# Attention with rotary embedding and a mixture of experts: the token lists' matrices are spread over four head pairs, built on ScalarE alone, with chunk counts summed by TensorE and token numbers taken from a constant table

## The chip, the cores and the metric

The kernel runs on one core of a Trainium2 chip. The metric is the device time of one execution in microseconds (us). A core has TensorE (PE; its weight loads are listed apart as PEld), VectorE (DVE), ScalarE (ACT), GpSimd (POOL) and SyncE (SP, which here only issues DMAs). Each engine works through its own instructions in the order in which the program gives them, and waits on semaphores for the other engines.

## The reference

Eight batches of 576 tokens go through attention with 8 heads of 64 columns; the result, 4608 tokens of 512 columns, goes through a mixture of experts in which each token visits one of 8 experts.

```python
q_rot, k_rot = rotate(q), rotate(k)                 # rotary embedding
scores = q_rot @ k_rot.T / sqrt(64)
attn = softmax(scores); x = attn @ v                # (8, 8, 576, 64) -> (4608, 512)
logits = x @ w_gate; e_idx = argmax(logits, axis=1)
gate_w = softmax(logits)[e_idx]; eom = sigmoid(x @ w_output_gate)
for e in range(8):
    mask = e_idx == e
    h = relu(x[mask] @ w1[e])
    out[mask] = gate_w[mask] * eom[mask, e] * (h @ w2[e])
```

## The kernel before, in words

**Attention.** Two heads form a pair; a batch has 4 pairs, the program 32. A pair is worked through in nine steps, one for each block of score rows (`STEPS`): steps 0 and 1, 2 and 3, 5 and 6, 7 and 8 are issued together, step 4 alone. A step multiplies the scores on TensorE (`score`, L509), takes the row peak and copies them out of PSUM on VectorE (`peak`, L518, tile `pm`), takes the exponential with its sum on ScalarE (`exp`, L525, tile `pm`) and turns them on VectorE (`turn`, L531 and L533, tile `pt`). One pair later the values are multiplied (L555, tile `acc`, one buffer for the whole kernel), ScalarE copies them out (`evict`, L562 to L564, tile `ac`), TensorE turns them back (`back`, L570, again into `acc`), and VectorE divides them into the rows of tokens (`divide`, L582, tile `xb`). GpSimd prepares the queries and keys of coming pairs: a multiplication by the rotary table (L460, two a pair), an addition (L464) and the low halves (L473).

**What sets the order.** A table of events gives each side task an offset in steps from the start of its pair, and a number that orders the tasks of one step; `step` issues a step's scores, peaks and exponentials, the turns of earlier steps, and then the tasks due. Nothing is reordered later: a task stands in its engine's queue between the exponentials, peaks or score products of the steps around it.

**The place of a token.** When a batch's four pairs are done, `place` finds for its tokens (5 chunks of 128, the last half full) the expert, the gate value, and the token's place in the expert's list. It runs 20 steps and more after the start of the batch's last pair, beside the attention of later pairs. `s0` to `s8` find the expert as a one-hot row per token (tile `oh`, a bf16 copy `ohb`). `add0` and `add` make sums of `ohb` over the chunks before (tile `ohs`). `s14` multiplies both by constant matrices on TensorE, which gives the rank of each token within its expert. `s15` to `s17` split the place into a row number `hr` and a column number `lo`. `ones(c)` and `places(c)` build for each chunk two matrices, `ro` (128x288, one where the row number agrees) and `pl` (128x128, the token's number where the column number agrees); on ScalarE each takes two activations, a square and a clipped difference (L736 and L737, L747 and L748). `s20` multiplies the five pairs of matrices into one bank of `acc` (L758), `s21` copies that out (L764, tile `lc`), and `s22` adds it to the lists on GpSimd. For the last batch all of this runs on VectorE, with pieces issued between the products of the experts.

Before the change, batches 0 to 5 have their ten matrices within offsets 25 to 40 (`ROWS`, `PLACES`), which is within a pair and a half; `pl` of chunks 0 to 2 is built on ScalarE (`TURNED` is 3), of chunks 3 and 4 on GpSimd (L750). Batch 6 (`ahead`) is placed while the attention ends.

**Experts.** Tokens are gathered by list in slots of 256 or 128, multiplied by both weight matrices of their expert (L1133, L1125, L1175) and scattered. This starts when attention ends and keeps TensorE busy to the end.

Of the kernel before, what the change touches and what calls it, by code (L numbers as in the profile page):

```python
# [22 lines left out]
E, FF = 8, 1024  # L23
# [49 lines left out]
C_E8, C_MASK, C_TOK, C_EB, C_SL, C_TRI, C_ONE, C_ROW = range(8)  # L73


def list_rows(nb):
# [13 lines left out]
    return n0, n2, max(min(E, most - 2 * p) + 2 * max(0, p - n2) for p in range(most // 2 + 1))  # L90


def const_table(nb):
# [11 lines left out]
    parts = [e8, mask, tok, eb, sl, tri, one, row]  # L105
# [160 lines left out]
class Attention:  # L266


    def __init__(self, tc, nb, pools, cc, ident, ii, first, trib, oneb, cnt, zero, qk, v, xd, row, lists):
# [32 lines left out]
        for i, pr in enumerate(self.pairs):  # L302
            g, b = 9 * i, i // NP
            fs = {"lasts": pr.lasts, "den0": pr.den0, "den1": pr.den1, "den2": pr.den2, "evict": pr.evict, "back": pr.back,
                  "newxb": lambda pr=pr, b=b: newxb(b) if pr.hp == 0 else None}
            fs["divide"] = lambda pr=pr, b=b: pr.divide(xbs[b])
            for t, n in ((slice(0, 1), "0"), (slice(1, 2), "1"), (slice(0, 2), "")):
                fs[f"mult{n}"] = lambda pr=pr, t=t: pr.mult("P", t)
                fs[f"add{n}"] = lambda pr=pr, t=t: pr.add("P", t)
                fs[f"hi{n}"] = lambda pr=pr, t=t: pr.high(t)  # L310
                fs[f"lo{n}"] = lambda pr=pr, t=t: pr.low("P", t)
            for t in range(2):
                fs[f"load{t}"] = lambda pr=pr, t=t: pr.load(t)
                fs[f"loadv{t}"] = lambda pr=pr, t=t: pr.loadv(t)
            for k, (b0, b1) in enumerate(PIECES):
                fs[f"av{k}"] = lambda pr=pr, b0=b0, b1=b1: [pr.values(j) for j in range(b0, b1)]
            for name, o, k in [*PREP.get(i, PREPARED), *EVENTS]:
                at(g + o, k, fs[name])
            if i % NP == NP - 1:
                fs = place(tc, (px, px2, small), self.pairs, b, NT, cc, trib, oneb, cnt, xbs, xd, row, lists, self.later)  # L320
# [70 lines left out]
class Pair:  # L391
# [194 lines left out]
def number(NT, b):

    m = NT // S // 2 * S
    return float(b * S - m + (b * S >= m))


def place(tc, pools, pairs, b, NT, cc, trib, oneb, cnt, xbs, xd, row, lists, later):
# [8 lines left out]
    T = {}  # L601

    def new(n, sh, dt=F32, **k):
        T[n] = p2.tile(sh, dt, tag=n, name=f"{n}{b}", **k)
        return T[n]

    sign = -1.0 if number(NT, b) < 0 else 1.0
    CE = [P, NCH, E]
    LO, LG = slice(0, E), slice(E, 2 * E)

# [30 lines left out]
    def s6():  # L641
# [18 lines left out]
    def add(c):  # L660
# [57 lines left out]
    def s17():  # L718
# [23 lines left out]
    def places(c):  # L742

        if c == 0:
            new("pl", [P, NCH, P], F32R, bufs=1)
        if not last and c < TURNED:
            nc.scalar.activation(T["pl"][:, c, :], row[:, 0:P], AF.Square, bias=T["lo"][:, c:c + 1], scale=-1.0)  # L747
            nc.scalar.activation(T["pl"][:, c, :], T["pl"].bitcast(F32)[:, c, :], AF.Relu, bias=T["tok"][:, c:c + 1], scale=T["tik"][:, c:c + 1])  # L748
            return
        V.tensor_scalar(T["pl"][:, c, :], row[:, 0:P], T["lo"][:, c:c + 1], T["tok"][:, c:c + 1], op0=ALU.is_equal,  # L750
                                op1=ALU.mult)

    def s20():

        T["ls"] = psum(4 if ahead else 5, 128, lists.shape[1])
        for c in range(NCH):
            m = QR if c == 4 else P
            nc.tensor.matmul(T["ls"], T["pl"][0:m, c, :], T["ro"][0:m, c, :], start=(c == 0), stop=(c == 4), skip_group_check=True)  # L758

    def s21():  # L760
        if last:
            nc.vector.tensor_tensor(out=lists, in0=lists, in1=T["ls"], op=ALU.subtract if sign < 0 else ALU.add)
            return
        nc.scalar.copy(new("lc", [P, lists.shape[1]], bufs=1), T["ls"])  # L764

    def s22():
        nc.gpsimd.tensor_tensor(out=lists, in0=lists, in1=T["lc"], op=ALU.subtract if sign < 0 else ALU.add)

    def both(f, c):
        return lambda: (f(), add(c))  # L770

    no = lambda: None
    if last:
        later += [lambda i=i: store(i) for i in range(3)]
        run = lambda *fs: lambda: [f() for f in fs]
        return [s0, run(s1, s2), s3, run(s4, s5), run(s6, s7), run(s8, add0), both(s9, 1), lambda: [add(c) for c in (2, 3, 4)],
                run(s10, s11, s12), run(s13, base), no, no, no, no, s14, no, s14b, run(s15, s16, s17)] + [
                lambda c=c: (ones(c), places(c)) for c in range(NCH)] + [no, no, s20, no, s21, no]

    def adds(*cs):  # L780
        return lambda: [add(c) for c in cs]
# [541 lines left out]
```

## Time and profile before

| | us |
|---|---|
| median of 3 runs (lowest, highest) | 974.33 (972.52, 975.57) |
| the profiled execution | 973.69 |
| its span, first to last instruction | 971.9 |

| engine | busy us | share of the span | instructions |
|---|---|---|---|
| PE | 910.4 | 94% | 14413 |
| DVE | 759.1 | 78% | 1353 |
| ACT | 650.2 | 67% | 1353 |
| POOL | 542.2 | 56% | 519 |

The shares are means over two stages with different limits. Attention lasts from the start to about 490 us, the experts from there to the end. [...] The number of tokens in a list depends on the data, which is the same in all runs.

### The profile page before, as it was taken

To read this page: it belongs to the slowest core of one execution; us is meant where nothing else is said; L and a number is where in the kernel's file an instruction comes from. 1 tells how busy PE (TensorE), PEld (TensorE's weight loads), DVE (VectorE), ACT (ScalarE), POOL (GpSimd) and SP (SyncE) were. 2 spreads that over 40 slices of the span, in tenths; PEclk is the share of its full clock that TensorE was granted. 3 is DMA by queue.
4 is the path that set the end of the run, shared out by engine and by line. 5 is a ranking of instruction groups with operands and counts; after the bars stand their busy time and mean duration, and the time that the engine had idled before them with its cause. 6 is when DMAs were issued, how large, how long until landed. Compare 5 with 4: busy or idle time off the path is not lost.

```text
span 971.9 us, 34146 instructions
## 1 busy us (share of the span) xinstructions
PE 910.4 (94%) x14413; PEld 787.9 (81%) x14413; DVE 759.1 (78%) x1353; ACT 650.2 (67%) x1353; POOL 542.2 (56%) x519
## 2 busy tenths in 40 slices
PE   4989989989899899889899999999999999999997
PEld 3768778767777777777788998999889998999986
DVE  6889989999899998999779767657665767658562
ACT  4767787897978878798765454446654756457561
POOL 5897889898898988898411222142514215142140
PEclk9999999999999999999999999999999999999999
DMA  6543563573564555562578877668786868868650
GB/s 234 198 168 132 195 223 138 196 253 114 217 209 177 204 195 180 182 225 91 209 297 281 305 238 236 210 201 303 258 288 223 301 201 279 283 225 286 197 202 23
DMA packets 57821, 208.38 MB, mean 214 GB/s; under 512 B 7946, under 2 KB 8252, under 8 KB 57664
## 3 DMA queue, kind: packets, MB, share of 16 engines
q1 hardware_dynamic: 49920, 183.78, 54.7%
q0 software_dynamic: 6464, 21.26, 5.9%
q8 instruction: 115, 1.88, 0.8%
q10 hardware_dynamic: 1280, 1.11, 0.3%
q14 instruction: 42, 0.34, 0.1%
HBM read 186.06 MB, written 22.43 MB: 215 GB/s over the span
## 4 chain that ended last, share of the span: by engine, by line
PE 43%; issue 4%; DVE 3%; ACT 2%; POOL 1%; DMA 1%; POOLq 0%; ACTq 0%; DVEq 0%
PE py L1175 19%; PE ph L1133 18%; PE ph L1125 3%; PE mtp L1098 1%; DVE wl L1092 1%; DMA out<-y,2idx 1%; ACT wh L1090 1%; PE acc L555 1%; PE htp L1160 0%; PE sc L509 0%; POOL kq L473 0%; POOL wl L1092 0%; POOLq L1254 0%; DVE ht L1150 0%; POOL out L1180 0%
## 5 line engine op out<-in xcount | busy, mean ns | idle before, releaser
L525 ACT ACTIVATE pm<-pm,m 128x576 f32<-128x576 f32 x288 | 221.7, 771 | 89.5 <-DVE pm L518 86.9
L1092 DVE TENSOR_TENSOR wl<-wr,wh 128x1024 fp32r<-128x1024 f32 x172 | 216.0, 1270 | 37.1 <-ACT wh L1090 34.2
L518 DVE TENSOR_SCALAR_CACHE_REDUCE pm<-sc 128x576 f32<-128x576 f32 x288 | 206.9, 750 | 26.3 <-PE sc L509 21.3
L555 PE MATMUL acc<-pt,v 32*64 32x160 f32 (+1 forms) x9216 | 197.2, 295 | 18.7 <-DVE xb L582 5.8
L1175 PE MATMUL py<-wh,ht 128*128 128x512 f32 x640 | 213.7, 399 | 0.0
L1133 PE MATMUL ph<-xt,wh 128*128 128x256 f32 x1088 | 197.3, 282 | 0.8 <-issue 0.4
L555 PEld LDWEIGHTS acc<-pt,v 32*64 32x64 f32 x9216 | 157.2, 131 | 44.1 <-issue 21.6
L1090 ACT CAST wh<-wr 128x1024 fp32r<-128x1024 f32 x184 | 187.8, 1049 | 0.0
L509 PE MATMUL sc<-kq 64*128 64x288 f32 x1536 | 156.6, 319 | 18.1 <-ACT kq L470 9.5
L1133 PEld LDWEIGHTS ph<-xt,wh 128*128 128x128 f32 x1088 | 168.6, 188 | 3.2 <-DVE xt L1114 1.8
L460 POOL TENSOR_TENSOR raw<-raw,rt 128x1152 f32<-128x1152 f32 x62 | 164.6, 2655 | 0.0
L509 PEld LDWEIGHTS sc<-kq 64*128 64x128 f32 x1536 | 118.7, 191 | 51.5 <-DVE pm L518 19.8
L1133 PE MATMUL ph<-xt,wl 128*128 128x256 f32 x544 | 153.5, 282 | 0.1
L1175 PEld LDWEIGHTS py<-wh,ht 128*128 128x128 f32 x640 | 120.4, 188 | 25.0
L533 DVE STREAM_TRANSPOSE pt<-pm 128x1152 f32<-128x1152 f32 x96 | 131.8, 1373 | 0.1
L1175 PE MATMUL py<-wl,ht 128*128 128x512 f32 x320 | 125.7, 393 | 0.0
L1180 POOL DMA_INDIRECT out<-y,2idx x24 | 28.1, 1169 | 163.8 <-ACT y L1189 103.5
L1149 ACT ACTIVATE ht<-ph 128x512 fp32r<-128x512 f32 x68 | 40.6, 597 | 109.0 <-PE ph L1133 106.6
L1133 PEld LDWEIGHTS ph<-xt,wl 128*128 128x128 f32 x544 | 102.2, 188 | 1.0 <-issue 0.5
L1150 DVE SCALAR_TENSOR_TENSOR ht<-ph,ht 128x512 fp32r<-128x512 f32 x68 | 46.9, 690 | 69.4 <-ACT ht L1149 65.3
L473 POOL TENSOR_TENSOR kq<-raw,kq 128x1152 fp32r<-128x1152 f32 (+1 forms) x33 | 82.5, 2500 | 10.9 <-ACT kq L470 10.7
L464 POOL TENSOR_TENSOR raw<-raw 128x1152 f32<-128x1152 f32 (+1 forms) x33 | 82.4, 2496 | 1.6
(251 smaller groups left out, 1112.0 us busy)
## 6 DMA issues: line engine op xcount, KB each, us to landing
wr<-in_w SPq DMA_DIRECT2D x184, 512.0 KB
raw<-in_qk SPq DMA_DIRECT2D x64, 576.0 KB
v<-in_v SPq DMA_DIRECT2D x64, 576.0 KB
xd<-xb SPq DMA_DIRECT2D x16, 640.0 KB
xd<-xb SPq DMA_DIRECT2D x8, 160.0 KB
rt<-in_rope ACTq DMA_DIRECT2D x1, 576.0 KB
xg<-xd,2idx POOLq DMA_INDIRECT x24, 6.5
out<-y,2idx POOLq DMA_INDIRECT x24, 3.9
```

Source lines behind the costliest of these rows:

```text
L460: self.eng(eng).tensor_tensor(out=rv, in0=rv, in1=rt, op=ALU.mult)
L464: self.eng(eng).tensor_tensor(out=r, in0=r, in1=self.sides(self.raw, t, 1, x), op=ALU.add)
L473: self.eng(eng).tensor_tensor(out=self.sides(self.kq, t, 0, x), in0=self.sides(self.raw, t, 0, x), in1=self.sides(self.kq.bitcast(F32), t, ...
L509: self.nc.tensor.matmul(self.ps[i][:, a, :HS], st, self.kq[r, mov, x], start=(n == 0), stop=(n == 2))
L518: self.nc.vector.tensor_scalar(self.halves(i), self.ps[i][:, :, :HS], 1.0, FAR, op0=ALU.mult, op1=ALU.min, accum_out=self.m[i])
L525: self.nc.scalar.activation(self.pc[i], self.pc[i], AF.Exp, bias=self.m[i], scale=-1.0, accum_out=self.z[:, zi:zi + 1])
L533: self.nc.vector.transpose(out=self.pt[:, c:c + 6:5, :], in_=self.pc[units])
L555: nc.tensor.matmul(self.acc[h * D:h * D + D, a, o:o + 32 * n], self.v[r, h, j, :], self.pt[r, u:u + n, 32 * j:32 * j + 32], start=(j == 0) ...
L1090: self.nc.scalar.copy(wh, r)
L1092: eng.tensor_tensor(out=wl, in0=r, in1=wh.bitcast(F32), op=ALU.subtract)
L1133: nc.tensor.matmul(ph[:, f, :], st[:, dc, fs], mv[:, dc, :], start=(n == 0), stop=(n == 11))
L1175: self.nc.tensor.matmul(py[h], st[:, f, hs], mv, start=(f == 0 and n == 0), stop=(f == 7 and n == 2))
```

## The change

Six edits, all in `place`, its tables of offsets and the constant table. First, a batch has a kind: `free` (batches 0 to 3), `late` (4), `early` (5), `ahead` (6), or it is the last (7). For the kinds free and late the matrices are spread: offsets 29 to 58 for free batches, 28 to 51 for the late one; the lists are multiplied two pairs later (free) or one pair later (late). Kinds early and ahead keep their offsets. Second, for free and late batches `pl` of all five chunks is built on ScalarE. Third, TensorE sums the chunk counts: five products of one chunk each with the matrix of ones, with the chunk's one-hot row broadcast over all later chunks, take the place of `add0`, `add` and one product. Fourth, token numbers `tok` and their negatives `tik` come from the constant table. Fifth, the one-hot rows are written as bf16 at once, into one tile `hot` shared by all batches (tile `score` likewise), and rows without a token are masked by the table `e8` and a ninth column of 0.5 in `score`. Sixth, `s3` to `s7` and `base` stand one to three steps later.

```diff
-LISTED = 44
-TURNED = 3
-ROWS, AHEAD, PLACES = (26, 29, 31, 35, 40), (26, 29, 29, 31, 31), (25, 29, 31, 34, 38)
+LISTED, LATE = 44, 9
+ROWS = {"ahead": (26, 29, 29, 31, 31), "early": (26, 29, 31, 35, 40), "late": (28, 33, 38, 42, 49), "free": (29, 38, 47, 51, 56)}
+PLACES = {"ahead": (26, 27, 28, 29, 30), "early": (25, 29, 31, 34, 38), "late": (29, 31, 40, 47, 51), "free": (33, 40, 42, 49, 58)}
+TURNED = {"ahead": 3, "early": 3, "late": NCH, "free": NCH}
...
-    mask = np.ones((P, NCH))
-    mask[QR:, NCH - 1] = 0.0
+    e8[QR:, (NCH - 1) * E:] = 0.0
...
-    tok = p + 128.0 * np.arange(NCH)[None, :]
+    tok = [s * sign(nb, b) * (p + 128.0 * np.arange(NCH)[None, :] + number(nb * S, b)) for b in range(nb) for s in (1.0, -1.0)]
...
+        self.tops = px.tile([P, NCH, E + 1], F32, name="score"), px.tile([P, NCH + 1, E], BF16, name="hot")
+        self.inits = [lambda t=t, x=x: nc.gpsimd.memset(t, x) for t, x in zip(self.tops, (0.5, 0.0))]
...
-        tt(out=new("oh", CE), in0=T["sc"], in1=b3(T["fx"]), op=ALU.subtract)
-        V.tensor_scalar(T["oh"], T["oh"], 0.0, None, op0=ALU.is_ge)
+        tt(out=new("od", CE), in0=score[:, :, 0:E], in1=b3(T["fx"]), op=ALU.subtract)
+        V.tensor_scalar(T["oh"], T["od"], 0.0, None, op0=ALU.is_ge)
...
-        tt(out=T["oh"], in0=T["oh"], in1=b3(cc(C_MASK)), op=ALU.mult)
...
-        V.tensor_copy(new("ohb", CE, BF16), T["oh"])
...
-        V.memset(ohs[:, 0, :], 0.0)
-        V.tensor_copy(ohs[:, 1, :], T["ohb"][:, 0, :])
...
-        tt(out=T["ohs"][:, c + 1, :], in0=T["ohs"][:, c, :], in1=T["ohb"][:, c, :], op=ALU.add)
...
-        nc.tensor.matmul(flat(rk), oneb, flat(T["ohs"]), start=True, stop=False, skip_group_check=True)
-        nc.tensor.matmul(flat(rk[:, 0:NCH, :]), trib, flat(T["ohb"]), start=False, stop=True, skip_group_check=True)
+        mm(rk, trib, hot, True, False)
+        for c in range(NCH):
+            mm(rk[:, c + 1:, :], oneb, hot[:, c:c + 1, :].broadcast_to((P, NCH - c, E)), False, c == NCH - 1)
...
-        V.tensor_scalar(new("tok", [P, NCH]), cc(C_TOK), sign, sign * number(NT, b), op0=ALU.mult, op1=ALU.add)
-        if not last:
-            V.tensor_scalar(new("tik", [P, NCH]), T["tok"], -1.0, None, op0=ALU.mult)
...
-        if not last and c < TURNED:
+        if not last and c < TURNED[kind]:
...
-        T["ls"] = psum(4 if ahead else 5, 128, lists.shape[1])
+        T["ls"] = psum((listed + PLACE) // 9 - 2, 128, lists.shape[1])
...
-    fs = [(0, 2, s0), (2, 2, s1), (2, 3, s2), (5, 2, s3), (8, 2, s4), (9, 2, s5), (10, 2, s6), (11, 2, s7), (12, 2, add0),
-          (12, 2, adds(1, 2)), (13, 2, adds(3, 4)), (6, 2, base), (15, 2, s8), (17, 2, s14), (17, 3, s14c), (19, 2, s14b), (18, 2, s9),
+    listed = LISTED + LATE * {"ahead": -1, "early": 0, "late": 1, "free": 2}[kind]
+    fs = [(0, 2, s0), (2, 2, s1), (2, 3, s2), (7, 2, base), (8, 2, s3), (10, 2, s4), (11, 2, s5), (12, 2, s7), (15, 2, s8), (17, 2, s14),
```

ScalarE's queue of the kernel before, in pair 8, steps 4 to 7, with the matrices of batch 0 (`pm` are the exponentials of the steps named by the number behind it, `ro` and `pl` the matrices, `ac` the copies of the values out of PSUM):

```order
L525 ACTIVATE pm_4_2364,z_111<-pm_4_2364,m_4_2372 128x576
L736 ACTIVATE ro_2302<-row,hr_2252 128x288
L737 ACTIVATE ro_2302<-ro_2302 128x288
L747 ACTIVATE pl_2290<-row,lo_2253 128x128
L748 ACTIVATE pl_2290<-pl_2290,tok_2259,tik_2261 128x128
L525 ACTIVATE pm_5_2415,z_111<-pm_5_2415,m_5_2430 128x576
L525 ACTIVATE pm_5_2415,z_111<-pm_5_2415,m_6_2432 128x576
L736 ACTIVATE ro_2302<-row,hr_2252 128x288
L737 ACTIVATE ro_2302<-ro_2302 128x288
L747 ACTIVATE pl_2290<-row,lo_2253 128x128
L748 ACTIVATE pl_2290<-pl_2290,tok_2259,tik_2261 128x128
```

The same place of a pair in the changed kernel, pair 9, the first with three groups of batch 0:

```order
L536 ACTIVATE pm_4_2638,z_117<-pm_4_2638,m_4_2646 128x576
L730 ACTIVATE ro_2397<-row,hr_2249 128x288
L731 ACTIVATE ro_2397<-ro_2397 128x288
L536 ACTIVATE pm_5_2691,z_117<-pm_5_2691,m_5_2706 128x576
L536 ACTIVATE pm_5_2691,z_117<-pm_5_2691,m_6_2708 128x576
L741 ACTIVATE pl_2536<-row,lo_2250 128x128
L742 ACTIVATE pl_2536<-pl_2536,ct 128x128
L553 COPY rz_114<-rz_114 64x1
L536 ACTIVATE pm_7_2759,z_117<-pm_7_2759,m_7_2774 128x576
```

Where two groups of two activations stood behind the exponential of step 4 and two behind that of step 6, one stands behind each now. A third stands behind the exponential of step 8 in the changed kernel; in pairs 8 and 10 to 11 the groups are set likewise, two or three a pair.

GpSimd's queue of the kernel before, in batch 0's `place` (`raw` and `kq` are the queries and keys of coming pairs, the rest are the small tiles named above):

```order
L642 TENSOR_TENSOR oh_1731<-oh_1731,ct 128x40
L460 TENSOR_TENSOR raw_1692<-raw_1692,rt 128x1152
L645 CAST ohb_1817<-oh_1731 128x40
L646 TENSOR_TENSOR t_1819<-oh_1731,lgs_1440 128x40
L473 TENSOR_TENSOR kq_1768<-raw_1401,kq_1768 128x2x576
L654 MEMSET ohs_1884 128x8
L655 COPY ohs_1884<-ohb_1817 128x8
L661 TENSOR_TENSOR ohs_1884<-ohs_1884,ohb_1817 128x8 x4
L460 TENSOR_TENSOR raw_1692<-raw_1692,rt 128x1152
```

The same stretch of the changed kernel:

```order
L638 TENSOR_SCALAR score<-dd_1530 128x5x8
L639 TENSOR_TENSOR score<-score,ct 128x5x8
L471 TENSOR_TENSOR raw_1689<-raw_1689,rt 128x1152
L646 TENSOR_TENSOR od_1815<-score,fx_1766 128x40
L647 TENSOR_SCALAR hot<-od_1815 128x40
L648 TENSOR_SCALAR sm_1768<-sm_1768 128x5
L484 TENSOR_TENSOR kq_1763<-raw_1405,kq_1763 128x2x576
L651 TENSOR_TENSOR t_1882<-hot,lgs_1444 128x40
L471 TENSOR_TENSOR raw_1689<-raw_1689,rt 128x1152
```

Of the small instructions between the large ones, the mask, the cast, the clearing, the copy and the four sums are gone, and the search for the expert (`score`, `od`, `hot`) stands one large instruction later.

## Rows read from the trace of the kernel before

**Rows 1.** Busy time by engine in two stretches: start:end, length, PE, PEld, DVE, ACT, POOL, clock, DMA
```profile
100.00:200.00 100.00, 91.09 (x2466) 75.34 (x2465) 92.92 (x192) 81.59 (x210) 89.31 (x90) 0.98 0.52 187
600.00:700.00 100.00, 100.00 (x644) 90.13 (x643) 64.82 (x78) 56.84 (x80) 31.29 (x20) 1.00 0.73 243
```

**Rows 2.** Timeline, VectorE: divisions of pairs 6 and 26 (start, length in us)
```profile
129.29 0.95 DVE L582 TENSOR_TENSOR xb<-acc,rz 128x800 f32<-128x800 f32 x1
...
420.37 0.95 DVE L582 TENSOR_TENSOR xb<-acc,rz 128x800 f32<-128x800 f32 x1
```

**Rows 3.** Busy time between divisions, pairs 5, 7 to 11, 27, 28
```profile
101.58:115.41 13.83, 12.88 (x356) 10.67 (x354) 13.35 (x29) 10.04 (x27) 13.19 (x17) 1.00 0.54 200
...
129.29:145.70 16.41, 13.67 (x349) 11.31 (x347) 13.52 (x27) 15.97 (x44) 14.28 (x8) 0.90 0.70 259
145.70:159.84 14.14, 13.77 (x362) 11.65 (x364) 13.63 (x30) 11.32 (x28) 12.82 (x13) 0.99 0.52 179
159.84:173.99 14.15, 13.12 (x362) 10.97 (x360) 13.35 (x29) 10.28 (x28) 13.51 (x18) 1.00 0.43 153
173.99:187.87 13.88, 12.80 (x356) 10.56 (x354) 13.40 (x30) 10.42 (x29) 11.50 (x15) 1.00 0.43 157
187.87:202.98 15.11, 12.37 (x349) 10.17 (x348) 13.43 (x27) 14.71 (x39) 14.27 (x8) 1.00 0.67 244
...
420.37:435.47 15.10, 12.38 (x349) 10.18 (x349) 13.43 (x27) 14.70 (x39) 14.45 (x15) 1.00 0.66 237
435.47:449.38 13.91, 13.63 (x362) 11.43 (x362) 13.62 (x33) 12.39 (x33) 13.45 (x19) 1.00 0.48 167
```

**Rows 4.** Timeline, TensorE: turning back in a crowded and a quiet pair; idle in brackets
```profile
142.63 3.03 PE L570 MATMUL acc<-ii,ac 128*128 128x160 f32 x10 [2.23 <-ACT ac L564]
...
171.16 1.62 PE L570 MATMUL acc<-ii,ac 128*128 128x160 f32 x10
```

**Rows 5.** Timeline, ScalarE: exponentials of steps 5, 7, 0 in a quiet pair
```profile
108.36 0.78 ACT L525 ACTIVATE pm<-pm,m 128x576 f32<-128x576 f32 x1 [1.30 <-DVE pm L518]
...
110.83 0.78 ACT L525 ACTIVATE pm<-pm,m 128x576 f32<-128x576 f32 x1 [0.63 <-DVE pm L518]
...
114.21 0.78 ACT L525 ACTIVATE pm<-pm,m 128x576 f32<-128x576 f32 x1 [0.69 <-DVE pm L518]
```

**Rows 6.** Groups, ScalarE: the matrices (busy us, mean ns | idle before)
```profile
L736 ACT ACTIVATE ro<-row,hr 128x288 fp32r<-128x288 bf16 x35 | 18.4, 526 | 0.3
L737 ACT ACTIVATE ro<-ro 128x288 fp32r<-128x288 f32 x35 | 15.6, 444 | 1.1
L748 ACT ACTIVATE pl<-pl,tok,tik 128x128 fp32r<-128x128 f32 x21 | 10.4, 494 | 1.1
L747 ACT ACTIVATE pl<-row,lo 128x128 fp32r<-128x128 bf16 x21 | 8.1, 386 | 0.0
```

**Rows 7.** Waits: TensorE's value products behind the lists' copy (total, times, longest)
```profile
PE acc L555 <- ACT lc L764: 4.6, 6, 1.0
```

**Rows 8.** Groups, GpSimd: the instructions that the change removes
```profile
L750 POOL TENSOR_SCALAR pl<-row,lo,tok 128x128 fp32r<-128x128 bf16 x14 | 11.3, 807 | 0.0
...
L661 POOL TENSOR_TENSOR ohs<-ohs,ohb 128x8 bf16<-128x8 bf16 x28 | 5.6, 200 | 2.1
...
L642 POOL TENSOR_TENSOR oh<-oh,ct 128x40 f32<-128x40 f32 x7 | 1.8, 254 | 0.5
L728 POOL TENSOR_SCALAR tik<-tok 128x5 f32<-128x5 f32 x7 | 1.7, 249 | 0.6
...
L726 POOL TENSOR_SCALAR tok<-ct 128x5 f32<-128x5 f32 x7 | 1.4, 197 | 0.3
```

**Rows 9.** Groups, TensorE: the product with the matrix of ones
```profile
L699 PE MATMUL acc<-ohs,oneb 128*128 128x48 bf16 x7 | 1.3, 186 | 0.5 <-POOL ohs L661 0.5
```

**Rows 10.** Timeline, pair 10: GpSimd's addition at step 0, VectorE's turn at step 2
```profile
158.37 2.67 POOL L464 TENSOR_TENSOR raw<-raw 128x1152 f32<-128x1152 f32 x1
...
162.09 1.37 DVE L533 STREAM_TRANSPOSE pt<-pm 128x1152 f32<-128x1152 f32 x1
```

More of the change, by code (lines that the diff above doesn't have):

```diff
@@ L70 @@
 FAR = 3.0e38
-C_E8, C_MASK, C_TOK, C_EB, C_SL, C_TRI, C_ONE, C_ROW = range(8)
+C_E8, C_TOK, C_EB, C_SL, C_TRI, C_ONE, C_ROW = range(7)
 def list_rows(nb):
@@ L90, in slot_counts, with number, sign @@
     return n0, n2, max(min(E, most - 2 * p) + 2 * max(0, p - n2) for p in range(most // 2 + 1))
+def number(NT, b):
+    m = NT // S // 2 * S
+    return float(b * S - m + (b * S >= m))
+def sign(nb, b):
+    return -1.0 if number(nb * S, b) < 0 else 1.0
 def const_table(nb):
@@ L103, in const_table @@
     row = np.tile(np.arange(E * list_rows(nb) // P) - MID, (P, 1))
-    tok = p + 128.0 * np.arange(NCH)[None, :]
-    parts = [e8, mask, tok, eb, sl, tri, one, row]
+    tok = [s * sign(nb, b) * (p + 128.0 * np.arange(NCH)[None, :] + number(nb * S, b)) for b in range(nb) for s in (1.0, -1.0)]
+    parts = [e8, np.concatenate(tok, 1), eb, sl, tri, one, row]
     offs = np.cumsum([0] + [a.shape[1] for a in parts])
@@ L319, in __init__ @@
             if i % NP == NP - 1:
-                fs = place(tc, (px, px2, small), self.pairs, b, NT, cc, trib, oneb, cnt, xbs, xd, row, lists, self.later)
+                fs = place(tc, (px, px2, small), self.pairs, b, NT, cc, trib, oneb, cnt, xbs, xd, row, lists, self.tops, self.later)
                 if b == nb - 1:
@@ L583, in divide, with place @@
                                      op=ALU.mult)
[L586 to L592, printed above, removed]
+def place(tc, pools, pairs, b, NT, cc, trib, oneb, cnt, xbs, xd, row, lists, tops, later):
     nc = tc.nc
@@ L600, in place @@
     b3 = lambda t: t.unsqueeze(2).broadcast_to((P, NCH, E))
-    T = {}
+    score, hot = tops
+    T = {"oh": hot[:, 0:NCH, :]}
     def new(n, sh, dt=F32, **k):
@@ L605, in new @@
         return T[n]
-    sign = -1.0 if number(NT, b) < 0 else 1.0
+    nb = NT // S
+    negative = sign(nb, b) < 0
+    kind = "ahead" if ahead else "early" if early else "late" if b == nb - 4 else "free"
+    tok, tik = (cc(C_TOK)[:, (2 * b + k) * NCH:(2 * b + k + 1) * NCH] for k in range(2))
     CE = [P, NCH, E]
@@ L745, in places @@
             new("pl", [P, NCH, P], F32R, bufs=1)
-        if not last and c < TURNED:
+        if not last and c < TURNED[kind]:
             nc.scalar.activation(T["pl"][:, c, :], row[:, 0:P], AF.Square, bias=T["lo"][:, c:c + 1], scale=-1.0)
-            nc.scalar.activation(T["pl"][:, c, :], T["pl"].bitcast(F32)[:, c, :], AF.Relu, bias=T["tok"][:, c:c + 1], scale=T["tik"][:, c:c + 1])
+            nc.scalar.activation(T["pl"][:, c, :], T["pl"].bitcast(F32)[:, c, :], AF.Relu, bias=tok[:, c:c + 1], scale=tik[:, c:c + 1])
             return
-        V.tensor_scalar(T["pl"][:, c, :], row[:, 0:P], T["lo"][:, c:c + 1], T["tok"][:, c:c + 1], op0=ALU.is_equal,
+        V.tensor_scalar(T["pl"][:, c, :], row[:, 0:P], T["lo"][:, c:c + 1], tok[:, c:c + 1], op0=ALU.is_equal,
                                 op1=ALU.mult)
     def s20():
-        T["ls"] = psum(4 if ahead else 5, 128, lists.shape[1])
+        T["ls"] = psum((listed + PLACE) // 9 - 2, 128, lists.shape[1])
         for c in range(NCH):
@@ L761, in s21 @@
         if last:
-            nc.vector.tensor_tensor(out=lists, in0=lists, in1=T["ls"], op=ALU.subtract if sign < 0 else ALU.add)
+            nc.vector.tensor_tensor(out=lists, in0=lists, in1=T["ls"], op=ALU.subtract if negative else ALU.add)
             return
@@ L766, in s22 @@
     def s22():
-        nc.gpsimd.tensor_tensor(out=lists, in0=lists, in1=T["lc"], op=ALU.subtract if sign < 0 else ALU.add)
-    def both(f, c):
-        return lambda: (f(), add(c))
+        nc.gpsimd.tensor_tensor(out=lists, in0=lists, in1=T["lc"], op=ALU.subtract if negative else ALU.add)
     no = lambda: None
+    listed = LISTED + LATE * {"ahead": -1, "early": 0, "late": 1, "free": 2}[kind]
     if last:
@@ L775, in place @@
         run = lambda *fs: lambda: [f() for f in fs]
[L776 to L781, printed above, removed]
-    fs = [(0, 2, s0), (2, 2, s1), (2, 3, s2), (5, 2, s3), (8, 2, s4), (9, 2, s5), (10, 2, s6), (11, 2, s7), (12, 2, add0),
-          (12, 2, adds(1, 2)), (13, 2, adds(3, 4)), (6, 2, base), (15, 2, s8), (17, 2, s14), (17, 3, s14c), (19, 2, s14b), (18, 2, s9),
-          (19, 2, lambda: (s10(), s11())), (20, 2, s15), (21, 2, s12), (22, 2, s16), (23, 2, s17)]
-    listed = LISTED - 9 if ahead else LISTED
+        return [s0, run(s1, s2), s3, run(s4, s5), s7, s8, s9, no, run(s10, s11, s12), run(s13, base), no, no, no, no, s14, no, s14b,
+                run(s15, s16, s17)] + [lambda c=c: (ones(c), places(c)) for c in range(NCH)] + [no, no, s20, no, s21, no]
+    fs = [(0, 2, s0), (2, 2, s1), (2, 3, s2), (7, 2, base), (8, 2, s3), (10, 2, s4), (11, 2, s5), (12, 2, s7), (15, 2, s8), (17, 2, s14),
+          (17, 3, s14c), (19, 2, s14b), (18, 2, s9), (19, 2, lambda: (s10(), s11())), (20, 2, s15), (21, 2, s12), (22, 2, s16), (23, 2, s17)]
     fs += [(listed, 2, s20), (listed, 3, s21), (listed + 1, 2, s22) if early else (listed + 2, 3, s22)]
-    fs += [((AHEAD if ahead else ROWS)[c], 3, lambda c=c: ones(c)) for c in range(NCH)]
-    fs += [(26 + c if ahead else PLACES[c], 3, lambda c=c: places(c)) for c in range(NCH)]
+    fs += [(ROWS[kind][c], 3, lambda c=c: ones(c)) for c in range(NCH)]
+    fs += [(PLACES[kind][c], 3, lambda c=c: places(c)) for c in range(NCH)]
     if b == NT // S - 2:
```

15 lines of the change are left out of this document (5 added, 10 removed).

## Prediction

> **What bounds the kernel now.** I read first the busy time by stretches, then the divisions on VectorE as milestones (one per pair), then the busy time between them, then the waits of the pairs that stand out.
>
> By stretches there are two stages [rows 1]. Among the experts TensorE is busy 100 us of 100, and nothing that another engine saves there counts. In attention VectorE has 92.9 us, TensorE 91.1, GpSimd 89.3 and ScalarE 81.6: no engine is full, so the mean names no bound.
>
> The divisions cut attention into pairs. I call an interval by the pair whose division ends it; the work in it is mostly that of the next pair. A quiet interval takes 13.83 us: VectorE is busy for 13.35 of them, ScalarE for 10.04 [rows 3]. So VectorE sets the quiet pace, with about half a microsecond of small waits. Interval 7 takes 16.41 us. VectorE has the same 13.52 of work there, but ScalarE has 15.97, with 44 instructions against 27: it is the bound. Interval 11 takes 15.11 us, with ScalarE at 14.71 [rows 3]. These are the pairs that hold the matrices of batches 0 and 1. I find the same in intervals 15, 19, 23 and 27: every fourth pair is crowded.
>
> What the crowding does is in one row: the exponentials queue behind the matrices, the copies of the values out of PSUM come late, and TensorE stands idle for 2.23 us before it turns them back. [...]
>
> The change touches the intervals in which batches 0 to 4 have their matrices, 7 to 26: 420.37 - 129.29 = 291.08 us for 20 intervals [rows 2]. At the 13.88 us of interval 10 they would take 277.6 [rows 3]. So 13.5 us is all that is to be had from them, 0.67 an interval.
>
> **The change part by part.**
>
> *The matrices spread.* A group is the two activations of one matrix: 526 + 444 = 970 ns for `ro`, 386 + 494 = 880 ns for `pl` [rows 6]. Before, a batch has 5 + 3 = 8 groups on ScalarE, 7.5 us within a pair and a half. After, it has 10, 9.25 us, in four pairs: two, three, three, two. A quiet pair has 10.04 us of ScalarE [rows 3], so a pair with three groups has about 10.04 + 2.8 = 12.8, and 13.1 with the small ones of `place`: under 13.88, but near.
>
> Where in the pair the groups stand decides, since ScalarE's queue keeps its order. Four of the ten stand behind the exponential of step 4, three behind step 6, three behind step 8. In a quiet pair ScalarE waits exactly there: 1.30 us before the exponential of step 5, 0.63 before step 7, 0.69 before step 0 of the next pair [rows 5]. The first place holds a group with room to spare. The other two are overrun by 0.88 - 0.63 = 0.25 and about 0.91 - 0.69 = 0.22 us. An exponential this late is not yet wanted: VectorE turns it only after the next two peaks, so a few tenths should be lost in the queue. I count a fifth of the overrun: 6 x 0.24 x 0.2 = 0.3 us a batch. That a pair can run at its pace with much of ScalarE filled is shown by interval 28, 13.91 us with 12.39 of ScalarE [rows 3]. Ends: none of it counts, or all, 1.4 us a batch.
>
> The late batch has four groups in its first pair, one of them behind step 2, and its lists multiplied in the fourth; I give it the same price.
>
> *What stays.* The lists are still multiplied in `acc`, and the next pair's value products wait for the copy `lc`, up to 1.0 us [rows 7]; that interval takes 14.15 instead of 13.88 [rows 3]. It is moved one or two pairs, not removed: 0.27 us a batch, 1.35 in all. Batch 5 keeps its crowded pair, interval 27 with 15.10 us [rows 3]; batch 6 is placed as before.
>
> *Work taken from GpSimd.* A free or late batch loses two `pl` of 807 ns, four sums of 200, the mask of 254, and `tok` and `tik` of 197 and 249 [rows 8]: 3.1 us, with the cast, the copy and the clearing left out. Batches 5 and 6 lose 1.5 each. GpSimd's work in intervals 8 to 11 is 12.82 + 13.51 + 11.50 + 14.27 = 52.1 us of 57.4 [rows 3]. After, it is 49 in 55.8. This is cover for the first part and nothing by itself, since GpSimd does not set the pace of a quiet pair: 13.88 us with 11.50 of GpSimd, 13.83 with 13.19 [rows 3]. Priced at 0; from 0 to -0.3 an interval.
>
> *Counts summed by TensorE.* Six products where there were two. One takes 186 ns from start to end [rows 9], so four more cost at most 0.75 us a batch, 6 for all eight, and nothing where they lie beside VectorE's work. In attention TensorE has 12.80 of 13.88 us [rows 3]; I take 0 there, and 0.3 for the last batch, which stands between the experts' products. VectorE loses nine small instructions for that batch; TensorE is the bound there, so I count nothing.
>
> [...]
>
> *Constants and clearing.* A larger table loaded once and two clearings at the start, beside the first loads: 0.
>
> *Steps moved.* The search for the expert starts three steps later and its result is wanted at the same step as before; the sums that stood between are gone. VectorE's two reductions `fx` and `sm` now come two steps behind GpSimd's `score`, before three. Behind them stand the peaks that set the pace, so a wait there would count in full. GpSimd's addition at step 0 ends at 161.0, `base` and `score` are three small instructions behind it (0.8 us at the mask's 254 ns [rows 8]), and VectorE reaches the reductions behind the turn that ends at 163.5 [rows 10]: 1.6 us to spare. Priced at 0.
>
> *Sum.* Before 291.08. After 277.6 + 1.35 + 5 x 0.3 = 280.4. The difference is 10.7, less 0.3 for the last batch: 10.4. The profiled execution took 973.69 us, so 963.3; the median of the three runs is 0.64 higher, and so is my forecast: 963.9 us.
>
> **Rivals.**
>
> *The overruns count in full* (0.12). ScalarE's queue keeps its order, so each group holds up all behind it. For it: a three-group pair leaves 0.8 us of ScalarE, and the copies out of PSUM stand right behind step 6's group. Against: interval 28. It costs 5 x (1.4 - 0.3) = 5.5 us more: 969.4.
>
> *GpSimd sets the pace* (0.10). With the crowded pairs gone GpSimd has fewer slow pairs in which to catch up; interval 9 has 13.51 of 14.15 us [rows 3]. For it: that is the fullest engine in any quiet pair. Against: three microseconds a batch are taken from it. If every interval took 14.15: 283.0 + 1.5, and the time is 968.
>
> *VectorE waits for GpSimd* (0.05), the other side. If GpSimd runs late by more than the 1.6 us that are to spare, `fx` and `sm` hold up the peaks. Late by one multiplication or addition (2.67 us [rows 10]) it costs 1.1 us, by two 3.7 a batch; from about 1.5 us a batch more than my sum over seven batches the gain is gone. By two: 963.9 + 7 x 3.7 = 990. For it: GpSimd has no idle time in interval 9. Against: its load falls.
>
> *The clock falls in batch 5's pair* (0.25, within my own case). Intervals 7 and 11 hold the same work and differ by 1.3 us and in clock, 0.90 against 1.00 [rows 3]; interval 27 is one without the fall. Interval 27 comes some 10 us earlier after the change and may turn into one with the fall: 963.9 + 1.3 = 965.2. [...]
>
> **How the numbers follow.** My own case has 0.70, a quarter of which (0.18) with the fall; the first two rivals 0.22, the third 0.05; 0.03 is left for more gain than I count (all 20 intervals at 13.83 and batch 5's pair at 13.9: 958). The range reaches from 960, where the overrun and the lists' wait cost nothing, to 969.5, the first rival. 0.3% is 2.9 us, about what a measurement of this kernel can tell from no change: faster means under 971.4. That holds in my case and in the first two rivals, short of their worst: 0.91. Slower by as much is the third rival, 0.05; 0.04 lies between.
>
> **What would show it.** In the profile after: no interval over 14.4 us among 7 to 26, ScalarE at 12 to 13.2 us in each, and VectorE again the fullest; TensorE's waits for `ac` of 2 us in one pair only, that of batch 5; the clock at 1.00 from 100 to 400 us; the experts' stage as long as before. Wrong would be: a steady 14.2 or more in the three-group intervals with TensorE waiting for `ac` or VectorE for the exponentials (first rival), GpSimd never idle with score products waiting for `kq` (second), VectorE waiting for `score` (third).

## The result, and the profile after

The changed kernel takes 963.57 us (median of 4 runs, 962.43 to 964.68), against 974.42 before (4 runs): a ratio of 0.9898, with a 95% interval of 0.9875 to 0.9922. 963.9 was predicted, within 960 to 969.5. The profiled execution took 962.43 us, with a span of 960.7.

The divisions on VectorE are the milestones again. These are the ones that end intervals 6 and 26 in the changed kernel, as in [rows 2] (start, length):

```profile
127.83 0.95 DVE L593 TENSOR_TENSOR xb<-acc,rz 128x800 f32<-128x800 f32 x1
...
408.21 0.95 DVE L593 TENSOR_TENSOR xb<-acc,rz 128x800 f32<-128x800 f32 x1
```

The 20 intervals between them take 280.38 us, against 291.08. Busy time in some of them (start:end, length, PE, PEld, DVE, ACT, POOL, granted clock with 1.00 as full speed, DMA share and GB/s), intervals 7 to 11, 19, 27 and 31, to be held against [rows 3]:

```profile
127.83:141.54 13.71, 13.03 (x356) 10.74 (x355) 13.23 (x27) 11.64 (x31) 12.88 (x6) 1.00 0.70 251
141.54:155.24 13.70, 12.96 (x356) 10.69 (x355) 13.30 (x28) 12.35 (x33) 12.43 (x9) 1.00 0.67 227
155.24:169.06 13.82, 13.08 (x362) 10.95 (x362) 13.46 (x31) 12.78 (x34) 12.35 (x12) 1.00 0.57 212
169.06:183.19 14.13, 13.03 (x359) 11.01 (x357) 13.39 (x29) 12.42 (x33) 10.59 (x14) 1.00 0.35 125
183.19:197.22 14.03, 12.95 (x358) 10.70 (x358) 13.23 (x27) 12.06 (x32) 13.33 (x7) 1.00 0.65 232
...
295.47:310.21 14.74, 12.68 (x355) 10.41 (x353) 13.34 (x28) 11.39 (x30) 13.46 (x7) 1.00 0.67 222
...
408.21:423.27 15.06, 12.60 (x349) 10.04 (x349) 13.40 (x27) 14.71 (x39) 14.37 (x16) 1.00 0.69 250
...
465.12:480.95 15.83, 12.41 (x336) 10.93 (x336) 6.91 (x9) 11.75 (x25) 1.26 (x2) 1.00 0.34 123
```

Interval 7 fell from 16.41 to 13.71 us. Its ScalarE has 11.64 us of work where it had 15.97, and the rest stands in the next three intervals, each with 12 to 13 us. VectorE is again the fullest engine, at 13.2 to 13.5 of some 13.9 (in interval 11 GpSimd is level with it). Batch 5's interval 27, left as it was, still takes 15.06. Two intervals were not in my account. Interval 19 took 14.74 us, with a pause of TensorE of 1.15 us in it; such pauses come below. Interval 31 grew to 15.83 us from 13.97, which in the kernel before was this one:

```profile
477.64:491.61 13.97, 13.14 (x336) 11.32 (x337) 7.01 (x10) 11.66 (x25) 2.54 (x5) 1.00 0.47 163
```

TensorE's waits before the turning back, for ScalarE's copies `ac`, first before and then after (total, times, longest):

```profile
PE acc L570 <- ACT ac L564: 14.5, 13, 2.2
```

```profile
PE acc L581 <- ACT ac L575: 5.6, 14, 1.3
```

The place of a group in the pair is seen in ScalarE's timeline of pair 10, in the changed kernel (start, length, in brackets the idle time before it):

```profile
159.83 0.78 ACT L536 ACTIVATE pm<-pm,m 128x576 f32<-128x576 f32 x1 [0.24 <-DVE pm L529]
...
160.60 0.52 ACT L730 ACTIVATE ro<-row,hr 128x288 fp32r<-128x288 bf16 x1
161.16 0.44 ACT L731 ACTIVATE ro<-ro 128x288 fp32r<-128x288 f32 x1
161.94 0.78 ACT L536 ACTIVATE pm<-pm,m 128x576 f32<-128x576 f32 x1 [0.34 <-DVE pm L529]
```

The 1.30 us of idle time of [rows 5] has become one group (0.96 us) and 0.34 us of idle time.

Where the 11.2 us of span come from: -1.5 before division 6, -10.7 in intervals 7 to 26, +1.5 in intervals 27 to 31, -0.5 among the experts.

### The profile page after: what moved, and what is told of

It reads as the page before. It is cut to its first block, busy times and chain, and to the rows that moved or that the text cites. A ratio compares the mean times of both kernels' runs of the same rounds, so it can differ in the third digit from the quotient of the medians.

```text
span 960.7 us, 34114 instructions
## 1 busy us (share of the span) xinstructions
PE 905.0 (94%) x14445; PEld 783.7 (82%) x14445; DVE 756.3 (79%) x1344; ACT 658.1 (69%) x1373; POOL 517.8 (54%) x441
## 3 DMA queue, kind: packets, MB, share of 16 engines
q8 instruction: 115, 1.88, 0.8%
q10 hardware_dynamic: 1280, 1.15, 0.4%
## 4 chain that ended last, share of the span: by engine, by line
PE 66%; DVE 16%; ACT 9%; issue 5%; DMA 2%; POOL 2%; POOLq 0%; DVEq 0%; SPq 0%; ACTq 0%
PE py L1161 20%; PE ph L1119 19%; PE acc L566 12%; PE sc L520 9%; DVE pm L529 8%; ACT pm L536 4%; DVE pt L544 4%; PE ph L1111 3%; PE mtp L1084 2%; DVE pt L542 1%; PE acc L581 1%; DVE xb L593 1%; DMA out<-y,2idx 1%; ACT bd L491 1%; DMA rt<-in_rope 1%
```

## The experiments

Each time stands beside runs of the kernel before on the same chip; a ratio is to those. The runs lie on three chips, so kernels that did not run side by side are compared by their ratios. The changed kernel's own ratio was 0.9898 above and 0.9922 in later runs.

**Only the spread.** The offsets, the list products and their bank of `acc` as in the change; everything else as before.

```diff
+ROWS = {..., "late": (28, 33, 38, 42, 49), "free": (29, 38, 47, 51, 56)}
+PLACES = {..., "late": (29, 31, 40, 47, 51), "free": (33, 40, 42, 49, 58)}
 TURNED = 3
...
-        T["ls"] = psum(4 if ahead else 5, 128, lists.shape[1])
+        T["ls"] = psum((listed + PLACE) // 9 - 2, 128, lists.shape[1])
...
+    listed = LISTED + LATE * {"ahead": -1, "early": 0, "late": 1, "free": 2}[kind]
```

> Only the spread of the matrices (and the lists multiplied later); pl of chunks 3 and 4, the sums over chunks, the mask and the token numbers stay on GpSimd. My theory, that the crowded queue of ScalarE was the loss, expects nearly the whole gain: 962 to 966 us, intervals 7 to 26 in 279 to 282 us. The rival, that GpSimd sets the pace once the crowded pairs are gone, expects 968 to 972, with intervals of 14.15 and more and GpSimd without idle time.

Measured: 964.02 us, ratio 0.9923 (0.9903 to 0.9943). This is the busy time of the whole stretch of intervals 7 to 26, of interval 9 and of interval 27, in this kernel:

```profile
127.89:408.32 280.43, 260.83 (x7079) 215.91 (x7078) 267.69 (x551) 240.08 (x621) 260.58 (x258) 1.00 0.55 197
...
155.63:169.46 13.83, 12.88 (x356) 10.66 (x354) 13.35 (x28) 11.88 (x31) 13.19 (x18) 1.00 0.55 206
...
408.32:424.27 15.95, 13.56 (x349) 11.07 (x345) 13.52 (x28) 15.55 (x42) 15.13 (x19) 0.93 0.66 246
```

The 20 intervals take 280.43 us, 0.05 more than in the changed kernel, although GpSimd keeps all its work: 260.58 us of 280.43, or 93%. The rival of GpSimd's pace falls. The spread is the whole gain in these intervals.

**All but the spread.**

```diff
-... "late": (28, 33, 38, 42, 49), "free": (29, 38, 47, 51, 56)}   (ROWS)
+... "late": (26, 29, 31, 35, 40), "free": (26, 29, 31, 35, 40)}
-... "late": (29, 31, 40, 47, 51), "free": (33, 40, 42, 49, 58)}   (PLACES)
+... "late": (25, 29, 31, 34, 38), "free": (25, 29, 31, 34, 38)}
-TURNED = {"ahead": 3, "early": 3, "late": NCH, "free": NCH}
+TURNED = {"ahead": 3, "early": 3, "late": 3, "free": 3}
...
-    listed = LISTED + LATE * {"ahead": -1, "early": 0, "late": 1, "free": 2}[kind]
+    listed = LISTED + LATE * {"ahead": -1, "early": 0, "late": 0, "free": 0}[kind]
```

> All edits but the spread: offsets, list products and pl of chunks 3 and 4 on GpSimd as in the kernel before. My theory expects no gain that can be told from none, 972 to 975.5 us, with 15.1 to 16.4 us in every fourth interval. The rival that work taken from GpSimd pays by itself expects 970 or less.

Measured: 973.56 us, ratio 1.0006 (0.9986 to 1.0027). The profile is of the longest of its 11 runs (981.25 us), with a span of 979.4 us; the crowded intervals are back in it. Intervals 7, 11 and 27:

```profile
131.03:146.88 15.85, 13.22 (x349) 10.83 (x345) 13.47 (x27) 15.51 (x42) 13.71 (x7) 0.94 0.69 235
...
189.58:205.93 16.35, 13.62 (x349) 11.33 (x347) 13.47 (x28) 15.97 (x44) 13.72 (x7) 0.91 0.71 260
424.39:441.59 17.20, 14.60 (x356) 12.04 (x355) 13.27 (x27) 15.12 (x39) 15.46 (x16) 0.90 0.69 240
```

Work taken from GpSimd, the products on TensorE, and the constants together bring nothing that these runs can tell from none (by the interval at most 0.14%, or 1.4 us, faster).

**Two `pl` on GpSimd.** The changed kernel with `"late": 3, "free": 3` in `TURNED`.

> The changed kernel, but pl of chunks 3 and 4 built on GpSimd as before (ScalarE 1.8 us a batch lighter, GpSimd 1.6 heavier). My theory, with VectorE as the pace and both others under it, expects 962.5 to 965 us, as the changed kernel. If the groups' overrun in ScalarE's queue counts it is faster by up to 1.4 us; if GpSimd is near the pace it is slower by 2 to 5 us.

Measured: 965.24 us, ratio 0.9936 (0.9912 to 0.9960); intervals 7 to 26 in 281.6. That is as much as the changed kernel beside other runs (0.9922, below) within the intervals. The median lies 0.24 us above the range that I had given. Which of the two engines builds these matrices makes no difference that the runs can tell.

**The same load, in one place.** The groups of each pair of the free batches stand together behind step 6; each pair has as many as in the changed kernel.

```diff
-... "free": (29, 38, 47, 51, 56)}
+... "free": (31, 40, 49, 49, 58)}
-... "free": (33, 40, 42, 49, 58)}
+... "free": (31, 40, 40, 49, 58)}
```

> The changed kernel, but in free batches all groups of a pair stand together behind the exponential of step 6 (two, three, three, two a pair, as many as in the changed kernel). If the place in the queue decides, the copies out of PSUM come 1.2 to 2.2 us late in 16 pairs, TensorE waits for ac in each, and the time is 971 to 985 us. If only ScalarE's load per pair counts it stays at 963 to 965.

Measured: 981.95 us, ratio 1.0099 (1.0080 to 1.0118): slower than before the change. Intervals 7 to 26 take 296.55 us. Intervals 8 and 9, and TensorE's turning back of a pair with three groups, in this kernel:

```profile
142.44:158.24 15.80, 13.42 (x354) 10.93 (x353) 13.51 (x29) 13.10 (x35) 14.46 (x13) 0.95 0.69 248
158.24:174.02 15.78, 13.69 (x360) 11.61 (x362) 13.69 (x30) 12.27 (x33) 10.24 (x8) 0.94 0.43 156
...
155.89 2.25 PE L581 MATMUL acc<-ii,ac 128*128 128x160 f32 x10 [2.00 <-ACT ac L575]
```

Interval 8 has 13.10 us of ScalarE in 15.80; interval 9 of the changed kernel has 12.78 in 13.82. The load is much the same, and the place in the queue decides: the copies `ac` come behind the groups, TensorE stands for 2.00 us, and the granted clock of the interval is 0.95. That is [rows 4] again. In the whole kernel these waits come to 26.0 us, against 5.6 in the changed one:

```profile
PE acc L581 <- ACT ac L575: 26.0, 19, 2.1
```

**Batch 5 spread too.** Its lists are wanted at the same time, but eight groups fit on the places where ScalarE waits.

```diff
-"early": (26, 29, 31, 35, 40)   (ROWS)
+"early": (26, 29, 33, 38, 42)
-"early": (25, 29, 31, 34, 38)   (PLACES)
+"early": (31, 35, 40, 34, 38)
```

> The changed kernel, with batch 5's matrices also at the three places in the pair where ScalarE waits (offsets 26, 29, 33, 38, 42 for ro, 31, 35, 40 for pl on ScalarE), lists multiplied when they were. If the same mechanism holds, interval 27 falls from 15.06 to 13.9 to 14.2 us and interval 28 stays under 14.2: 962 to 963 us. If the pair is slow for another reason it stays at 15 us and the time at 963.5.

**Sums on GpSimd.** The changed kernel with `add0`, `add` and two products in place of six.

```diff
...
-        mm(rk, trib, hot, True, False)
-        for c in range(NCH):
-            mm(rk[:, c + 1:, :], oneb, hot[:, c:c + 1, :].broadcast_to((P, NCH - c, E)), False, c == NCH - 1)
+        mm(rk, oneb, T["ohs"], True, False)
+        mm(rk[:, 0:NCH, :], trib, T["oh"], False, True)
...
```

> The changed kernel, but the sums over chunks on GpSimd again and two products on TensorE instead of six. My theory of what the six products cost: the wait for rc grows by 0.2 to 0.3 us a batch, and the longer code of TensorE puts a load of code, a pause of 1.8 to 2.4 us, into interval 31; so interval 31 at 14 to 14.8 instead of 15.8 us, and 960.5 to 962.5 in all. The rival, that the four sums on GpSimd cost as much, expects 963 to 966.

**Both.** The two edits above together.

> The two before together: batch 5's matrices spread, sums on GpSimd. If they add up: 959 to 962 us, the fastest version. If the sums matter on GpSimd in batch 5's pairs: 963 or more.

**The changed kernel again**, beside these three.

> The changed kernel once more, beside these three on the same chip. Expected 962.5 to 965 us. If the pause in interval 31 is a load of code at a fixed place of TensorE's program, it is there again between the same two products, of any length; if it was chance, interval 31 takes 14 us.

| kernel, same chip | us | ratio to before (95%) |
|---|---|---|
| before | 972.01 | |
| changed again | 965.02 | 0.9922 (0.9901 to 0.9943) |
| batch 5 spread too | 963.90 | 0.9924 (0.9896 to 0.9953) |
| sums on GpSimd | 960.97 | 0.9879 (0.9856 to 0.9902) |
| both | 958.46 | 0.9858 (0.9834 to 0.9882) |

Batch 5's crowded pair did nearly what was expected. Intervals 27 and 28 with batch 5 spread, first with the sums on TensorE, then (next fence) with both edits:

```profile
410.91:425.22 14.31, 13.22 (x356) 10.55 (x356) 13.24 (x28) 13.13 (x35) 13.59 (x16) 1.00 0.66 244
425.22:438.97 13.75, 13.00 (x357) 10.92 (x355) 13.46 (x30) 13.26 (x35) 13.37 (x15) 1.00 0.55 189
```

```profile
410.61:424.32 13.71, 12.99 (x356) 10.73 (x356) 13.23 (x28) 13.04 (x35) 13.06 (x16) 1.00 0.66 239
424.32:438.07 13.75, 13.24 (x357) 10.97 (x356) 13.46 (x30) 13.35 (x36) 13.37 (x15) 1.00 0.57 204
```

15.06 us became 14.31 and 13.71, with 13 us of ScalarE. But interval 29 grew. It is shown in the changed kernel, with batch 5 spread, and with both edits:

```profile
437.18:451.33 14.15, 13.25 (x366) 11.10 (x364) 13.54 (x30) 10.38 (x29) 10.42 (x22) 1.00 0.28 102
```

```profile
438.97:454.00 15.03, 13.18 (x366) 11.11 (x364) 13.68 (x30) 10.97 (x29) 11.24 (x23) 1.00 0.30 108
```

```profile
438.07:453.80 15.73, 13.05 (x355) 10.70 (x353) 13.76 (x31) 11.44 (x30) 12.17 (x28) 1.00 0.29 106
```

With both edits TensorE waits in it 1.2 us for the lists' copy `lc` and 0.7 us for `kq` from GpSimd, where it waits 0.7 and 0.2 in the changed kernel. So the three intervals 27 to 29 together take 43.1, 43.1 and 43.2 us: what was won in the crowded pair was paid two pairs later. As a single edit the medians show no gain either (963.90 against 965.02, with runs from 961.67 to 969.09). With both edits the kernel takes 958.46 us: faster than the one before by 13.6 us, and than the changed one, whose runs all lie 4 us and more above its runs.

The sums on GpSimd brought about 4 us, but not in the way that I had written. The wait for `rc` stayed. This is TensorE's wait in the changed kernel, then with the sums on GpSimd (total, times, longest):

```profile
PE acc L566 <- ACT rc L701: 6.3, 7, 1.1
```

```profile
PE acc L566 <- ACT rc L708: 6.2, 7, 1.1
```

So it is not the length of the six products; `rc` is copied by ScalarE. Nor did interval 31 fall to the 14 to 14.8 us that I had expected: it took 15.66, with a pause of 1.90 us and a granted clock of 0.89. Most of the gain stands where I had not looked for it, among the experts. From the last division to the end, first the changed kernel, then with the sums on GpSimd:

```profile
480.95:960.70 479.75, 473.65 (x3072) 427.65 (x3072) 317.16 (x449) 265.21 (x363) 129.59 (x93) 1.00 0.71 245
```

```profile
483.32:960.30 476.98, 471.12 (x3068) 425.85 (x3068) 317.86 (x455) 265.23 (x363) 129.95 (x93) 1.00 0.72 246
```

These 2.7 us are there in each of the three profiles with this edit (477.0 to 477.1 us), and in none of the seven with the sums on TensorE (479.7 to 479.9). It is not the number of products, since the kernel before, with as few, took 480.29. TensorE is idle for under 1 us there until its last product; the same products follow each other a little faster, and why is not shown.

**TensorE's program shifted.** 100 tiny products (28 in the second kernel, which is the one with both edits) at the start of TensorE's program move all its later instructions on.

```diff
+    pad = small.tile("pad")
+    for _ in range(100):
+        nc.tensor.matmul(pad[0:32, 0, 0:8], ident[:, 0:32], ident[:, 0:8], start=True, stop=True, skip_group_check=True)
```

> The changed kernel with 100 tiny products (32x8, f32) at the start of TensorE's program, before the first score product, where TensorE waits for its inputs anyway; their result is used by nothing. They move every later instruction of TensorE 100 products further on in its program. If the pauses without a releaser are loads of code at fixed places of the program, the two in interval 31 stand elsewhere (one place, behind 42 value products of the last pair but one, as in the kernel before) and the time falls by 1 to 3 us, to a ratio of 0.989 to 0.991 against 0.9922. If the pauses belong to the work, they stand where they stood, and the ratio stays at 0.992 or rises.

> The fastest version so far (early spread, sums on GpSimd) with 28 tiny products at the start, which gives its attention end the alignment of the changed kernel. If the place of the code loads matters, pauses stand behind 14 and 142 value products as in the changed kernel and the ratio rises from 0.9858 by 0.001 to 0.004; if not, it stays at 0.985 to 0.987.

First the pauses. TensorE in interval 31 of the changed kernel, and (second fence) in its second profile:

```profile
468.55 0.51 PE L566 MATMUL acc<-pt,v 32*64 32x160 f32 x14
471.44 2.44 PE L566 MATMUL acc<-pt,v 32*64 32x160 f32 x128 [2.38 <-issue]
474.91 0.75 PE L566 MATMUL acc<-pt,v 32*64 32x160 f32 x18 [1.03 <-issue]
```

```profile
471.25 0.51 PE L566 MATMUL acc<-pt,v 32*64 32x160 f32 x14
473.33 2.44 PE L566 MATMUL acc<-pt,v 32*64 32x160 f32 x128 [1.56 <-issue]
477.35 0.75 PE L566 MATMUL acc<-pt,v 32*64 32x160 f32 x18 [1.58 <-issue]
```

The profile shows nothing that is waited for ("issue"). The pauses stand behind product 14 and product 142 both times, and their lengths differ. With 100 products ahead the same stretch runs through:

```profile
475.65 1.09 PE L1087 MATMUL mtp<-ident,xg 128*128 128x128 f32 x8
476.67 3.00 PE L569 MATMUL acc<-pt,v 32*64 32x160 f32 x160
```

Interval 31 takes 13.76 us there, at a granted clock of 0.89 and with the DMA engines busy for 0.19 of the time (0.34 in the changed kernel). I had expected one pause behind product 42, and there is none. But the shift was not what I had meant: the profile shows each tiny product twice, 200 in the first kernel and 56 in the second:

```profile
1.38 10.83 PE L176 MATMUL pad<-ident 128*32 128x8 f32 x200 [1.38 <-POOL ident masks.py:199]
```

```profile
1.37 3.16 PE L176 MATMUL pad<-ident 128*32 128x8 f32 x56 [1.37 <-POOL ident masks.py:199]
```

The kernel with both edits has its pause in this stretch behind product 41, of 1.88 us. A shift of 56 with a step of 128 puts it behind 113, and there it stands in the second padded kernel:

```profile
471.25 2.25 PE L569 MATMUL acc<-pt,v 32*64 32x160 f32 x113
476.10 1.07 PE L569 MATMUL acc<-pt,v 32*64 32x160 f32 x47 [2.61 <-issue]
```

Counted through the whole program, padding included, a pause stands behind product 11,188 or 11,316 (give or take one) in eleven of the twelve profiles; the first padded kernel is the one without. So the pauses belong to places in TensorE's program and not to the work; whether a place pauses, and for how long, differs from run to run. The pause of 1.15 us in interval 19 is one of them:

```profile
306.60 0.53 PE L566 MATMUL acc<-pt,v 32*64 32x160 f32 x16 [1.15 <-issue]
```

The times did not follow. The padded changed kernel takes 967.28 us, ratio 0.9941 (0.9918 to 0.9963), not to be told from 0.9922. The tiny products took 10.8 us and delayed the first score product to 12.1 us from 9.5, and in interval 30 ScalarE paused for 2.38 us before a copy of `ac`, with 17.79 us for the interval and a granted clock of 0.89. The second kernel takes 961.48 us, ratio 0.9885 (0.9861 to 0.9908), 0.0027 above the unpadded one; some 1.1 us of that is the later start (first division at 44.81 against 43.73). What the placing of the code is worth in all stays open.

## Why the prediction was right

**What bounds.** Right: ScalarE in the crowded pairs, VectorE elsewhere. The experiment with the groups in one place shows that it is ScalarE's order and not its load: TensorE's waits for `ac` went from 14.5 to 5.6 us with the change and to 26.0 with the groups together.

**The matrices spread.** 280.4 us predicted for intervals 7 to 26, 280.38 measured. The agreement to that digit is luck, for two terms were off against each other. The quiet pace is 13.7 us and not 13.88 (intervals 7 and 8). Against that stand waits of TensorE that I had priced low or not at all: intervals with `rc` take 14.13 us and not 13.88, since `rc` comes later in ScalarE's fuller queue. The overrun of the groups did not count in intervals 7 to 9: 13.7 to 13.8 us. And the second profile of the changed kernel, from its later runs, has 283.41 us for the same intervals: there a pause of 1.44 us fell into interval 24, which took this long at a granted clock of 0.91:

```profile
366.91:382.60 15.69, 13.74 (x349) 11.28 (x347) 13.49 (x29) 13.19 (x35) 14.34 (x13) 0.91 0.64 218
```

So the sign "no interval over 14.4 us" failed in both profiles (14.74 in the first), by a wait that the prediction did not know.

**What stays.** Right for the lists' copy (interval 11, 14.03 us) and for batch 5 (15.06).

**GpSimd.** Priced at 0, and 0 it was: the spread alone brings the same 280.4. The rival of GpSimd's pace and the one of VectorE waiting for `score` did not come. (The prediction's 57.4 us for intervals 8 to 11 should be 57.3, and its 958 us for the largest gain nearer 959; nothing hangs on either.)

**TensorE's six products.** Their own time was priced rightly at nothing in attention. Missed was that a longer program meets its pauses elsewhere: interval 31 took 1.9 us more, with two pauses of 3.4 us together. That the length of the program is what these 1.9 us cost is not shown: with the sums on GpSimd, in a program as long as before, the interval took 15.66 us and 14.04 in the two profiles.

**The clock.** Batch 5's pair kept 1.00 in the changed kernel and took 15.06 us. The same pair had 0.93 and 15.95 us with the spread alone, and 0.90 and 17.20 us in the profile of the kernel without the spread. Its work was not laid out quite alike in the three kernels, and what decides whether the clock falls is not shown; the 0.25 that I gave to the fall was an estimate. From 100 to 400 us the clock is 1.00, where it was 0.98; in the second profile of the changed kernel it is 0.99.

The clock of 0.90 in interval 7 of the kernel before is a mean: it was 1.00, with one stretch of 3.41 us at 0.50. Two more of the same length begin at 258.50 and 374.55 us, in intervals 15 and 23 (fourth and fifth line):

```profile
129.29:142.46 13.17, 10.61 (x337) 8.58 (x335) 11.49 (x23) 12.79 (x34) 13.07 (x7) 1.00 0.64 233
142.46:145.87 3.41, 3.24 (x12) 2.91 (x14) 2.19 (x6) 3.35 (x11) 1.20 (x2) 0.50 0.89 355
145.87:151.00 5.13, 5.13 (x155) 4.30 (x157) 4.90 (x9) 3.93 (x8) 4.06 (x4) 1.00 0.03 11
258.50:261.91 3.41, 3.30 (x12) 2.98 (x14) 2.19 (x6) 3.35 (x11) 1.13 (x2) 0.50 0.91 355
374.55:377.96 3.41, 3.41 (x14) 3.08 (x16) 2.19 (x6) 3.37 (x10) 1.03 (x2) 0.50 0.79 301
```

The slow turning back of [rows 4], which has TensorE's 2.23 us of idle time just before it, lies whole in the first of them.

**The end.** The experts took 479.75 us from the last division on, against 480.29 before; I had counted 0.3 us more for the last batch, not 0.5 less.

**The total.** That 963.57 us came so close to 963.9 is partly luck. Outside intervals 7 to 26 the span changed by -1.5, +1.5 and -0.5 us where the sum has +0.3. The first two cancel, and both go with pauses of TensorE. In intervals 1 and 2 the kernel before lost 2.5 us to three of them (this is the longest) and the changed kernel 0.5 us to two; in interval 31 it was the other way round, 0.7 us against 3.4.

```profile
66.60 0.77 PE L555 MATMUL acc<-pt,v 32*64 32x128 f32 x23 [1.20 <-issue]
```

## What to carry to other kernels

Look at a periodic stage period by period before believing its mean: ScalarE had 82% on average and was the bound in every fourth pair. On an engine with an ordered queue, side work belongs behind the instructions after which that engine waits anyway; the same work in another place of the same pair cost some 18 us (981.95 against 964.02 for the spread alone, on the same chip). Once a crowded stretch is found, look for all of its kind, but add up the stretches behind it too: the one that was left (batch 5) became 0.8 to 1.4 us shorter, and a later one grew by about as much.

## What the runs showed of the hardware

TensorE pauses at fixed places of its program: in eleven of the twelve profiles behind product 11,188 or 11,316, as counted above. The pauses there last from 0.3 to 2.7 us, in kernels of 14,400 products, and the two places are 128 products apart. The page of the profile lists a queue for instructions:

```profile
q8 instruction: 115, 1.88, 0.8%
```

In the trace each of these packets has 16,384 bytes. If the queue carries TensorE's program alone, the 14,445 products of the changed kernel and as many weight loads come to 251 a packet, which is an estimate from the page; 128 products and their weight loads are 256. Few packets cost time: the first profile of the changed kernel has nine pauses (6.2 us) before value products, and 89 packets before attention ends. At the end of attention the cost is higher: the two pauses together took 3.4 and 3.1 us in the two profiles.

The trace holds these packets one by one. In the first profile a packet of this queue landed at 470.05 us and the next at 473.57; the products started again at 471.44 and 474.91. The profile of the kernel before and the first of the changed one have 19 pauses ("issue") before attention ends, of 0.2 to 2.4 us; 17 end so, 1.3 to 1.5 us after a packet has landed, and the four of 1 us or more are among them. From this I read the pauses as late loads of the program; which instructions a packet holds is not shown.

What lies before a pause differs within the pair. In the 3 us before the first one the DMA engines were busy for 0.95 of the time, and its packet set out at 469.05 us, when the products stopped. In the second pause they were idle. Its packet set out 1.1 us after the first pause had ended, took 1.0 us, and was used 1.3 us after landing, while the 128 short products between the two pauses last 2.44 us: here TensorE was through its products 1.03 us before it went on.
